# The filler of an attention kernel: hidden units of the MLP dealt between thirds of its second product

## The chip, the cores and the metric

The program runs on one core of one Trainium2 chip. The metric is the device time of one execution in microseconds. An execution of the kernel before was also profiled; the profile holds every instruction of the five engines: TensorE (PE, with its weight loads shown as PEld), VectorE (DVE), ScalarE (ACT), GpSimd (POOL) and SyncE (SP, which issues all DMAs here).

## The reference

`x` is 2048 rows of 640. The rows are normalised, `xn`; attention and an MLP read the same `xn`, and the result joins both:

```python
xn = _layernorm(x, axis=-1)
s = _A_ref(xn, A_wqkv, A_wo)                      # 32 heads of 20, causal window of 256, softmax, then @ wo
g = _silu(_B_ref(xn, B_w1, B_b1, B_w2, B_b2))     # relu(xn @ w1 + b1)**2 @ w2 + b2, hidden width 1536
return x + s * g
```

## The kernel before

All products are done in fp16 with operands split in a high and a low part (high x high, high x low, low x high), so that each product takes three matmuls per tile of the contraction.

**Stages.** A first stage (lines 195 to 529) normalises and transposes x, makes the values of all heads and the first of five groups of 128 q/k rows (each group serves 6.4 heads). Then comes the main loop of 269 steps: 16 pairs of heads times 16 blocks of 128 rows, plus 13 steps in which the last blocks run out. Step s computes the scores of block s (`scores`, L557, 4 matmuls `sps`), their row maxima on DVE (`maxima`, L568), ten steps later the transposed scores (`scores_t`, L604, 4 matmuls `stps` into the one PSUM tile that there is for them), the exponential on ACT (`exps`, L609) with two masking instructions on POOL (L610, L612), one step later its fp16 high part on ACT (`high`, L617), then the low part on DVE (`low`, L623), and every second step 24 small matmuls with the values (`values`, L637, `ops`; 12 of them in the first two blocks of a pair of heads). Last, a tail after the loop does the output product (`out_filler`, tiles `wops`).

**The filler.** The attention of a step leaves TensorE free for most of the step. A generator, `filler()`, gives one matmul at a time with an estimated cost, and `fill(amount)` takes matmuls from it twice in each step until the costs catch up with an even share: `total_` is 423.4 us of cost over 268 steps, 1.58 us a step. The order of the instructions on each engine is the order in which the program issues them (`manual_schedule`), so the order inside `filler()` is the order on TensorE. The filler's work, in this order:

1. q/k groups 1 to 4: for each group g, four column blocks b, and for each of q and k one product of 15 matmuls of 512 columns (`qkps`, cost 0.218 each): 32 units. Each is evacuated by one ACT and one DVE instruction (`qk_parts`, L80 and L81, tile `shm`) and stored by two DMAs.
2. For each of 8 blocks n of 256 rows: 12 hidden units `fc` of 15 matmuls of 256 columns (`hps`, cost 0.111 each), each evacuated by ACT relu (L855), ACT square (L856, tile `hh` high part), DVE square (L858) and POOL subtraction (L859, `hh` low part); then the second product, for two row tiles `tt` and two halves `nh` 36 matmuls of 320 columns (`yps`, cost 0.138 each), evacuated by one DVE instruction (L886).
3. The output product.

Between the hidden units and the second product of a block stands a `flush()`, which issues all evacuations that are pending. Evacuations of a finished product are otherwise pending until the flush in the middle of the next step.

**Weights on the way.** `piece` queues a load of 128 rows of weights into one of `RAW` = 3 buffers and a conversion (`split_s`, L125 on ACT, L126 on DVE) that `tick()` issues at most once a step; a tag in `shut` holds its conversions back, and `ensure(tag)` finishes them at once. Group g + 1 is queued while group g is computed. 17 pieces (`queue_squares`) give sums of squares for the scales of w2 and wo; `second_scales` needs them; then `queue_w2(0)`, `(1)` and, near the end of the q/k groups, `(2)` queue the 12 pieces of w2. w2 lies in three tiles of the pool `bigp`, which has 10 buffers; the third becomes free when the q/k weights `qkw` are no longer read. `queue_wo` queues the five pieces of wo at the start of the last block.

**Buffers.** PSUM pool `pmm` has three banks, shared by `qkps`, `hps` and `yps`. Pool `stgp` has `STG` = 10 buffers, shared by `shm` and the `hh` pairs (two hidden units in one buffer, so six for a block).

Of the kernel before, what the change touches and what calls it, by code (L numbers as in the profile page):

```python
# [7 lines left out]
F32 = mybir.dt.float32  # L8
I32 = mybir.dt.int32
BF16 = mybir.dt.bfloat16  # L10
F16 = mybir.dt.float16
AF = mybir.ActivationFunctionType
# [11 lines left out]
NB = 4  # L24
# [10 lines left out]
LAG = 10  # L35
PB = 6
RATE = 0.9
STG = 10
RAW = 3
EARLY_FILL = 0.35  # L40
SWING = 0.3
# [16 lines left out]
def attn_mlp_kernel(ctx: ExitStack, tc, x, wqkv, wo, w1, b1, w2, b2, out):  # L58
# [20 lines left out]
    def qk_parts(hm, ps):  # L79
        nc.scalar.activation(hm[:, 0, :], ps, AF.Copy, scale=QK_DOWN)  # L80
        nc.vector.scalar_tensor_tensor(hm[:, 1, :], ps, QK_DOWN, hm[:, 0, :], ALU.mult, ALU.subtract)  # L81
# [77 lines left out]
    def lin1(tiles, off, n):  # L159
        t, o = divmod(off, SLOT)  # L160
        return tiles[t][:, o:o + n]
# [370 lines left out]
    at1 = ctx.enter_context(tc.tile_pool(name="at1", bufs=1))  # L532
    qs.append(at1.tile([P, S], F16, name="qs1"))
    ks.append(at1.tile([P, S], F16, name="ks1"))
    at4 = ctx.enter_context(tc.tile_pool(name="at4", bufs=PB))
    at2 = ctx.enter_context(tc.tile_pool(name="at2", bufs=2))

# [125 lines left out]
    def post(dst, src):  # L663
        posts.append((dst, src))
# [9 lines left out]
    def mark():  # L674
        return flushed[0] + len(pending)
# [9 lines left out]
    def mm_group(ps, mms, cost):  # L685
        n = len(mms)
        for j, (a, b_) in enumerate(mms):
            nc.tensor.matmul(ps, a, b_, start=j == 0, stop=j == n - 1)  # L688
            yield cost
# [54 lines left out]
    def ensure(tag):  # L744
        flush()
        while any(p[0] == tag for p in started) or any(p[0] == tag for p in queue):
            start_pieces()
            for f in release(1, True):
                f()
                held[0] -= 1  # L750
# [21 lines left out]
    def queue_squares():  # L772
        for acc, src in [(ss2[:, f:f + 1], w2[f * P:(f + 1) * P, :]) for f in range(NF)] + [(sso[:, c:c + 1], wo[c * P:(c + 1) * P, :]) for c in range(KC)]:
            def go(raw, acc=acc):
                nc.scalar.activation(unread, raw, AF.Square, accum_out=acc)
            piece("s", src, go)

    def weighted_squares():
        g2 = col("m_g2", NF)
        nc.gpsimd.tensor_mul(g2, ss2, mlp["ic4"])  # L780
        mlp["g2"] = g2

    def second_scales():
        s2, i2 = weight_scale("w2", totals("w2_t", pmm.tile([P, NF], F32, tag="mm", name="sums2"), mlp["g2"]))
        so, io = weight_scale("wo", totals("wo_t", pmm.tile([P, KC], F32, tag="mm", name="sumso"), sso))
        sf = col("m_sf", NF)
        nc.vector.tensor_scalar(sf, mlp["ic2"], s2, None, ALU.mult)
        iw = col("o_inv")
        nc.gpsimd.tensor_mul(iw, io, mlp["iv"])
        nc.gpsimd.tensor_scalar(iw, iw, 1.0 / (XS * V_DOWN), 1.0, ALU.mult, ALU.mult)  # L790
        mlp.update(s2=sf, i2=i2, so=so, io=iw)
# [3 lines left out]
    def queue_w2(j):  # L795
        def go(raw, f):
            if len(w2t) == j:
                w2t.append(bigp.tile([P, SLOT], F16, tag="big", name=f"w2_{j}"))
            hi, lo = (lin1(w2t, (2 * f + q) * D, D) for q in range(2))
            split_s(hi, lo, raw, mlp["s2"][:, f:f + 1])  # L800
        for f in range(4 * j, 4 * j + 4):
            piece(f"2{j}", w2[f * P:(f + 1) * P, :], lambda raw, f=f: go(raw, f))

    def filler():
        ws = {1: {w: tuple(qkw[0][:, 1, i, j] for j in range(2)) for i, w in enumerate("qk")}}
        for g in range(1, KC):
            ensure(f"g{g}")
            for b in range(NB):
                if g + 1 < KC and b == 0:
                    ws[g + 1] = queue_group(g + 1)  # L810
                    shut.add(f"g{g + 1}")
                if b == 1:
                    shut.discard(f"g{g + 1}")
                    if g == 1:
                        queue_squares()
                if g == KC - 2 and b == 2:
                    ensure("s")
                    weighted_squares()
                if g == KC - 2 and b == 3:
                    second_scales()  # L820
                    queue_w2(0)
                    queue_w2(1)
                if g == KC - 1 and b == 2:
                    queue_w2(2)
                    shut.add("22")
                for w in "qk":
                    hi, lo = ws[g][w]
                    ps = pmm.tile([P, BT], F32, tag="mm", name="qkps")
                    yield from mm_group(ps, [(wt[:, c, :], xT[b][:, part, c, :]) for c in range(KC) for wt, part in ((hi, 0), (hi, 1), (lo, 0))], 0.218)

                    def evac(ps=ps, w=w, g=g, b=b):
                        hm = stg.tile([P, 2, BT], F16, tag="stg", name="shm")
                        qk_parts(hm, ps)
                        posts.extend(qk_stores(w, slice(g * P, (g + 1) * P), slice(b * BT, (b + 1) * BT), hm))
                    pending.append(evac)
        shut.discard("22")
        nblk = S // MT
        for n in range(nblk):
            if n == nblk - 1:
                wo_part = queue_wo()  # L840
                shut.add("o")
            xb = xT[n // 2][:, :, :, n % 2 * MT:(n % 2 + 1) * MT]
            hs = []
            for fc in range(NF):
                ps = pmm.tile([P, MT], F32, tag="mm", name="hps")
                yield from mm_group(ps, [(lin1(w1t, (2 * c + wp) * F + fc * P, P), xb[:, xp, c, :]) for c in range(KC) for wp, xp in ((0, 0), (0, 1), (1, 0))], 0.111)
                if fc % 2 == 0:
                    pair = stg.tile([P, 2, 2, MT], F16, tag="stg", name="hh")
                hh = pair[:, fc % 2]
                hs.append(hh)  # L850

                def evac(ps=ps, hh=hh, fi=fc):
                    at_f = slice(fi, fi + 1)
                    r = at2.tile([P, MT], F32, tag="relu", name="relu")
                    nc.scalar.activation(r, ps, AF.Relu, bias=mlp["bc"][:, at_f], scale=mlp["a"][:, at_f])  # L855
                    nc.scalar.activation(hh[:, 0], r, AF.Square)  # L856
                    sq = at2.tile([P, MT], F32, tag="sq", name="sq")
                    nc.vector.tensor_mul(sq, r, r)  # L858
                    nc.gpsimd.tensor_sub(hh[:, 1], sq, hh[:, 0])  # L859
                pending.append(evac)  # L860
            if n == nblk - 1:
                shut.discard("o")
            flush()
            if n == 0:
                for j in range(3):
                    ensure(f"2{j}")
            for tt in range(2):
                t = n * 2 + tt
                ysb = wgt.tile([P, D], F32, tag="ysb", name="ysb")
                pss = [pmm.tile([P, HALF], F32, tag="mm", name="yps")]  # L870
                steps_ = []
                for nh in range(2):
                    sl = slice(nh * HALF, (nh + 1) * HALF)
                    for fc in range(NF):
                        steps_.append((max(fc - NF + 3, 0) if tt == 0 else 0, nh, fc, sl))
                if tt == 0:
                    steps_.sort(key=lambda z: z[0])
                for _, nh, fc, sl in steps_:
                    if nh and len(pss) == 1:
                        pss.append(pmm.tile([P, HALF], F32, tag="mm", name="yps"))  # L880
                    for j, (hp, wp) in enumerate(((0, 0), (0, 1), (1, 0))):
                        nc.tensor.matmul(pss[nh], hs[fc][:, hp, tt * P:(tt + 1) * P], lin1(w2t, (2 * fc + wp) * D + nh * HALF, HALF), start=fc == 0 and j == 0, stop=fc == NF - 1 and j == 2)  # L882
                        yield 0.138

                    def evac(ps=pss[nh], ysb=ysb, sl=sl, nh=nh, t=t):
                        nc.vector.scalar_tensor_tensor(ysb[:, sl], ps, mlp["i2"], b2t[:, sl], ALU.mult, ALU.add)  # L886
                        if nh:
                            post(y_d[:, t, :], ysb)
                    if fc == NF - 1:
                        pending.append(evac)  # L890
                if n == nblk - 1:
                    load(0)
                    load(1)
        ensure("o")
        yield from out_filler(wo_part)

# [203 lines left out]
```

## Time and profile before

| | |
|---|---|
| median of 3 runs | 849.37 us (849.28 to 849.63) |
| the profiled execution's own time | 848.83 us |
| its span, first to last instruction | 847.0 us |
| main loop, first to last exponential | 141.5 to 762.2 us |
| q/k groups 1 to 4 on TensorE | 118.9 to 281.2 us |
| hidden units and second products | 281.2 to 767.5 us |
| output product and end | 767.5 to 847.0 us |
| busy time of PE, DVE, ACT, POOL | 822.7, 692.8, 648.1, 485.0 us |

The busy time of a matmul in these records runs from its start to a modelled end, so that consecutive matmuls overlap and a stage can show TensorE busy throughout though its matmuls stand further apart than they need. The distance from start to start is the better measure; the prediction works with it. A row of the stage view reads: the stretch, its length, then for each engine the busy microseconds and the number of instructions, the granted TensorE clock, the DMA engines' busy share and GB/s.

### The profile page before, as it was taken

Reading aid. Unit: us, or ns where it says so; the run is one execution under the profiler, and the core shown is the slowest. Engines: PE = TensorE matmul, PEld = TensorE weight load, DVE = VectorE, ACT = ScalarE, POOL = GpSimd, SP = SyncE. Lnnn points to the kernel's source line nnn. Section 1 sums busy time; section 2 is a strip of 40 time slices with the busy share of each in tenths; the row PEclk is TensorE's granted clock in tenths of the full one; section 3 lists DMA queues with packets and bytes.
Section 4 is the critical chain, followed back from the end, with each engine's and each line's share of the span. In section 5 each row is a group of like instructions: output and inputs, shape, how many; then the busy total and the mean of one; then the engine's idle time right before and its main releaser. Section 6 shows DMA issues by size and latency. Waiting matters only on the chain.

```text
span 847.0 us, 25061 instructions
## 1 busy us (share of the span) xinstructions
PE 822.7 (97%) x9426; PEld 553.4 (65%) x9426; DVE 692.8 (82%) x1897; ACT 648.1 (77%) x1028; POOL 485.0 (57%) x874
## 2 busy tenths in 40 slices
PE   8999998999999999999999999999999999999998
PEld 7765553444444676776766766766767767767775
DVE  6776566788999998898988998888988888975655
ACT  5565446998898997897997997987987988993321
POOL 2000001456665798796896986886986977961000
PEclk9999999999999999999999999999999999999999
DMA  7994349755475311213111222113122113055883
GB/s 245 250 349 129 135 127 283 234 162 157 127 229 163 111 44 55 66 33 89 51 49 50 65 52 65 50 33 84 30 76 65 49 42 99 11 180 171 301 297 126
DMA packets 100498, 104.52 MB, mean 123 GB/s; under 512 B 42520, under 2 KB 72856, under 8 KB 100376
## 3 DMA queue, kind: packets, MB, share of 16 engines
q1 hardware_dynamic: 100376, 102.91, 39.8%
q8 instruction: 74, 1.21, 0.6%
q14 instruction: 48, 0.39, 0.2%
HBM read 65.67 MB, written 36.83 MB: 121 GB/s over the span
## 4 chain that ended last, share of the span: by engine, by line
PE 60%; ACT 14%; POOL 8%; DVE 7%; issue 6%; DMA 3%; SPq 1%; DVEq 0%; ACTq 0%; POOLq 0%
PE yps L882 17%; PE wops L688 8%; PE vps L292 7%; PE hps L688 6%; ACT p L609 5%; PE ops L637 5%; PE qkps L688 5%; PE sps L557 4%; ACT ph L617 3%; PE qkps L503 3%; DVE junk L568 3%; PE stps L604 2%; POOL hh L859 2%; DVE pl L623 2%; ACT relu L855 2%
## 5 line engine op out<-in xcount | busy, mean ns | idle before, releaser
L609 ACT ACTIVATE p<-stps,ebias,esc 128x768 f32<-128x768 f32 (+2 forms) x256 | 242.1, 946 | 59.7 <-PE stps L604 48.9
L568 DVE CUSTOM_DVE_ANT_0 junk<-sps,mask 128x320 bf16<-128x320 f32 (+2 forms) x512 | 220.8, 468 | 49.0 <-PE sps L557 41.4
L623 DVE TENSOR_TENSOR pl<-p,ph 128x768 f16<-128x768 f32 (+2 forms) x256 | 248.8, 972 | 3.8 <-ACT ph L617 3.2
L610 POOL TENSOR_SCALAR_AFFINE_SELECT p<-p 128x256 f32<-128x256 f32 x256 | 163.8, 640 | 86.0 <-ACT p L609 76.7
L617 ACT ACTIVATE ph<-p 128x768 f16<-128x768 f32 (+2 forms) x256 | 203.1, 793 | 2.4 <-POOL p L612 1.6
L688 PE MATMUL hps<-xT,w 128*128 128x256 f16 x1440 | 176.2, 273 | 0.0
L882 PE MATMUL yps<-w,hh 128*128 128x320 f16 x1152 | 174.6, 300 | 0.0
L688 PEld LDWEIGHTS <-w 128*128 128x128 f16 x1440 | 132.6, 98 | 36.0 <-issue 17.2
L882 PEld LDWEIGHTS <-hh 128*128 128x128 f16 x1152 | 104.7, 98 | 57.0 <-issue 18.1
L688 PE MATMUL qkps<-xT,qkw 128*128 128x512 f16 x480 | 115.4, 380 | 0.5 <-DVE w_t L153 0.5
L612 POOL TENSOR_SCALAR_AFFINE_SELECT p<-p 128x256 f32<-128x256 f32 x224 | 103.6, 463 | 0.0
L557 PE MATMUL sps<-ks,qs 60*64 60x320 f16 (+2 forms) x1024 | 87.4, 312 | 6.8 <-DVE mt L568 5.9
L637 PE MATMUL ops<-vp,ph 128*128 128x41 f16 x1440 | 89.8, 181 | 0.0
L637 PE MATMUL ops<-vp,pl 128*128 128x41 f16 x1440 | 89.5, 180 | 0.0
L637 PEld LDWEIGHTS <-ph 128*128 128x128 f16 x1440 | 84.5, 96 | 6.2 <-issue 0.6
L604 PE MATMUL stps<-qs,ks 62*64 62x320 f16 (+4 forms) x1024 | 80.9, 293 | 6.7 <-ACT p L609 6.1
L573 POOL CAST mp<-mt 128x8 f16<-128x8 f32 x64 | 44.6, 698 | 70.0 <-DVE mt L568 69.7
L637 PEld LDWEIGHTS <-pl 128*128 128x128 f16 x1440 | 78.9, 96 | 5.6
L859 POOL TENSOR_TENSOR hh<-sq,hh 128x256 f16<-128x256 f32 x96 | 74.9, 782 | 6.4 <-DVE sq L858 4.3
L688 PEld LDWEIGHTS <-qkw 128*128 128x128 f16 x480 | 41.6, 98 | 55.4 <-issue 11.7
L292 PE MATMUL vps<-wv,xT 128*128 128x320 f16 x480 | 70.3, 303 | 3.2 <-ACT xT L261 1.6
L557 PEld LDWEIGHTS <-qs 60*64 60x64 f16 x1024 | 32.5, 103 | 55.2 <-issue 47.4
(150 smaller groups left out, 1032.4 us busy)
## 6 DMA issues: line engine op xcount, KB each, us to landing
ks<-k_d SPq DMA_DIRECT2D x64, 120.0 KB
qs<-q_d SPq DMA_DIRECT2D x64, 120.0 KB
raw<-in_B_w_dram SPq DMA_DIRECT2D x24, 320.0 KB
v_d<-vt SPq DMA_DIRECT2D x8, 656.0 KB
vp<-v_d SPq DMA_DIRECT2D x16, 328.0 KB
xt<-in_A_x_dram SPq DMA_DIRECT2D x16, 320.0 KB
k_d<-shm SPq DMA_DIRECT2D x20, 256.0 KB
q_d<-shm SPq DMA_DIRECT2D x20, 256.0 KB
```

Source lines behind the costliest of these rows:

```text
L292: nc.tensor.matmul(ps, xT[b][:, xp, c, t * P:(t + 1) * P], wv[wp][:, c, nh * HALF:(nh + 1) * HALF], start=n == 0, stop=n == 3 * KC - 1)
L557: nc.tensor.matmul(ps[HB * j:HB * (j + 1), :nk], qs[i][rows_, q0:q0 + HB], ks[i][rows_, k0:k0 + nk], start=True, stop=True)
L568: nc.vector.tensor_tensor_reduce(out=junk[:, :nk], in0=ps[:, :nk], in1=mk, scale=1.0 / MAX_UNIT, scalar=-3.0e38, op0=ALU.add, op1=ALU.max, ...
L604: nc.tensor.matmul(ps[HB * j:HB * (j + 1), hh, c0:c1], ks[i][rows_, kb * P + HB * j:kb * P + HB * (j + 1)], qs[i][rows_, kb * P + c0:kb * ...
L609: nc.scalar.activation(p32[:, :, :n], ps[:, :, :n], AF.Exp, scale=esc[0], bias=ebias)
L610: nc.gpsimd.affine_select(p32[:, :, 0:P], p32[:, :, 0:P], pattern=[[0, 2], [1, P]], compare_op=ALU.is_ge, fill=0.0, base=0, channel_multip ...
L612: nc.gpsimd.affine_select(p32[:, :, 2 * P:], p32[:, :, 2 * P:], pattern=[[0, 2], [-1, P]], compare_op=ALU.is_gt, fill=0.0, base=0, channel ...
L617: nc.scalar.activation(ph[:, :, :n], p32[:, :, :n], AF.Copy)
L623: nc.vector.tensor_sub(pl[:, :, :n], p32[:, :, :n], ph[:, :, :n])
L637: nc.tensor.matmul(ot[:, q % 4, hh, :], t[:, hh, (q - k) * P:(q - k + 1) * P], vp[:, k // 4, k % 4, hh, :], start=m == 1, stop=m == 2 * le ...
L688: nc.tensor.matmul(ps, a, b_, start=j == 0, stop=j == n - 1)
L882: nc.tensor.matmul(pss[nh], hs[fc][:, hp, tt * P:(tt + 1) * P], lin1(w2t, (2 * fc + wp) * D + nh * HALF, HALF), start=fc == 0 and j == 0, ...
```

## The change

The filler becomes a list of units that is built first and run in that order:

- the first 16 q/k units (groups 1 and 2) come alone, as before;
- the other 16 (groups 3 and 4) alternate with the 12 hidden units of block 0;
- then the 12 hidden units of block n + 1 alternate with 12 *thirds* of the second product of block n (a third is 12 of the 36 matmuls of one accumulation: four of the twelve `fc`), so that an accumulation stays open in its PSUM bank while hidden units run between its thirds;
- the last block's second product comes alone.

Each unit's matmuls and evacuation are the same as before. Before a third, the evacuations are flushed as far as the hidden units that it reads. The pool of staging buffers goes from 10 to 12. The third w2 tile gets a pool of its own (`w2p`), so that all 12 w2 pieces are queued together, after `second_scales`; `weighted_squares` and `second_scales` come at column blocks 0 and 1 of group 3 in place of 2 and 3. `load(0)` and `load(1)` are called ahead of every unit of the last second product.

```diff
-STG = 10
+STG = 12
...
+    w2p = ctx.enter_context(tc.tile_pool(name="w2p", bufs=1))
...
-                w2t.append(bigp.tile([P, SLOT], F16, tag="big", name=f"w2_{j}"))
+                w2t.append(w2p.tile([P, SLOT], F16, name=f"w2_{j}") if j == 2 else bigp.tile([P, SLOT], F16, tag="big", name=f"w2_{j}"))
...
+    def group_unit(g, b, w):
...
+            if g == KC - 2 and b == 0:
+                ensure("s")
+                weighted_squares()
+            if g == KC - 2 and b == 1:
+                second_scales()
+                for j in range(3):
+                    queue_w2(j)
...
+    def out_unit(n, tt, nh, third):
...
+        fs = range(third * THIRD, (third + 1) * THIRD)
+        flush(ready_h[n, fs[-1]])
+        if third == 0:
+            if nh == 0:
+                outs[t] = wgt.tile([P, D], F32, tag="ysb", name="ysb")
+            outs[t, nh] = pmm.tile([P, HALF], F32, tag="mm", name="yps")
+        ps, ysb = outs[t, nh], outs[t]
+        for fc in fs:
+            hh = hidden[n, fc // 2][:, fc % 2]
+            for j, (hp, wp) in enumerate(((0, 0), (0, 1), (1, 0))):
+                nc.tensor.matmul(ps, hh[:, hp, tt * P:(tt + 1) * P], lin1(w2t, (2 * fc + wp) * D + nh * HALF, HALF), start=fc == 0 and j == 0, stop=fc == NF - 1 and j == 2)
+                yield 0.138
...
+    def merge(*lists):
+        items = [((k + 0.5) / len(l), i, u) for i, l in enumerate(lists) for k, u in enumerate(l)]
+        return [u for _, _, u in sorted(items, key=lambda z: z[:2])]
+
+    def filler():
+        groups = [(group_unit, g, b, w) for g in range(1, KC) for b in range(NB) for w in "qk"]
+        hid = [[(hidden_unit, n, fc) for fc in range(NF)] for n in range(nblk)]
+        mlp2 = [[(out_unit, n, tt, nh, third) for tt in range(2) for nh in range(2) for third in range(3)] for n in range(nblk)]
+        half = len(groups) // 2
+        units = groups[:half] + merge(groups[half:], hid[0])
+        for n in range(nblk - 1):
+            units += merge(hid[n + 1], mlp2[n])
+        units += mlp2[-1]
+        for u in units:
+            if u[:3] == (hidden_unit, nblk - 1, 0):
                 wo_part = queue_wo()
                 shut.add("o")
...
+            if u[:2] == (out_unit, nblk - 1):
                 shut.discard("o")
...
+                load(0)
+                load(1)
+            yield from u[0](*u[1:])
```

More of the change, by code (lines that the diff above doesn't have):

```diff
@@ L802, in queue_w2 @@
             piece(f"2{j}", w2[f * P:(f + 1) * P, :], lambda raw, f=f: go(raw, f))
[L804 to L809, printed above, removed]
+    nblk = S // MT
+    hidden, ready_h, outs = {}, {}, {}
+    ws = {1: {w: tuple(qkw[0][:, 1, i, j] for j in range(2)) for i, w in enumerate("qk")}}
+    def group_unit(g, b, w):
+        if w == "q":
+            if b == 0:
+                ensure(f"g{g}")
+                if g + 1 < KC:
@@ L810, in filler @@
                     ws[g + 1] = queue_group(g + 1)
                     shut.add(f"g{g + 1}")
[L812 to L839, printed above, removed]
+            if b == 1:
+                shut.discard(f"g{g + 1}")
+                if g == 1:
+                    queue_squares()
+            if g == KC - 2 and b == 0:
[5 more added lines that the diff above has]
+                    queue_w2(j)
+        hi, lo = ws[g][w]
@@ new lines, in group_unit, with evac, hidden_unit @@
+        ps = pmm.tile([P, BT], F32, tag="mm", name="qkps")
+        yield from mm_group(ps, [(wt[:, c, :], xT[b][:, part, c, :]) for c in range(KC) for wt, part in ((hi, 0), (hi, 1), (lo, 0))], 0.218)
+        def evac():
+            hm = stg.tile([P, 2, BT], F16, tag="stg", name="shm")
+            qk_parts(hm, ps)
+            posts.extend(qk_stores(w, slice(g * P, (g + 1) * P), slice(b * BT, (b + 1) * BT), hm))
+        pending.append(evac)
+    def hidden_unit(n, fc):
+        xb = xT[n // 2][:, :, :, n % 2 * MT:(n % 2 + 1) * MT]
+        ps = pmm.tile([P, MT], F32, tag="mm", name="hps")
+        yield from mm_group(ps, [(lin1(w1t, (2 * c + wp) * F + fc * P, P), xb[:, xp, c, :]) for c in range(KC) for wp, xp in ((0, 0), (0, 1), (1, 0))], 0.111)
+        def evac():
+            if fc % 2 == 0:
+                hidden[n, fc // 2] = stg.tile([P, 2, 2, MT], F16, tag="stg", name="hh")
+            hh = hidden[n, fc // 2][:, fc % 2]
+            at_f = slice(fc, fc + 1)
+            r = at2.tile([P, MT], F32, tag="relu", name="relu")
+            nc.scalar.activation(r, ps, AF.Relu, bias=mlp["bc"][:, at_f], scale=mlp["a"][:, at_f])
+            nc.scalar.activation(hh[:, 0], r, AF.Square)
+            sq = at2.tile([P, MT], F32, tag="sq", name="sq")
+            nc.vector.tensor_mul(sq, r, r)
+            nc.gpsimd.tensor_sub(hh[:, 1], sq, hh[:, 0])
+        pending.append(evac)
+        ready_h[n, fc] = mark()
@@ new lines, in attn_mlp_kernel, with evac @@
+    THIRD = NF // 3
+    def out_unit(n, tt, nh, third):
+        if (n, tt, nh, third) == (0, 0, 0, 0):
+            for j in range(3):
+                ensure(f"2{j}")
+        t = n * 2 + tt
+        sl = slice(nh * HALF, (nh + 1) * HALF)
+        fs = range(third * THIRD, (third + 1) * THIRD)
[6 more added lines that the diff above has]
+        for fc in fs:
+            hh = hidden[n, fc // 2][:, fc % 2]
+            for j, (hp, wp) in enumerate(((0, 0), (0, 1), (1, 0))):
+                nc.tensor.matmul(ps, hh[:, hp, tt * P:(tt + 1) * P], lin1(w2t, (2 * fc + wp) * D + nh * HALF, HALF), start=fc == 0 and j == 0, stop=fc == NF - 1 and j == 2)
+                yield 0.138
+        def evac():
+            nc.vector.scalar_tensor_tensor(ysb[:, sl], ps, mlp["i2"], b2t[:, sl], ALU.mult, ALU.add)
+            if nh:
+                post(y_d[:, t, :], ysb)
+        if third == 2:
+            pending.append(evac)
@@ L840, in filler @@
                 wo_part = queue_wo()
                 shut.add("o")
[L842 to L860, printed above, removed]
@@ L861, in filler @@
-            if n == nblk - 1:
-                shut.discard("o")
[L863 to L893, printed above, removed]
```

## The prediction

> **What bounds the kernel now.** I read the page's head first, then the stretches of the loop, the timeline of TensorE inside two of them, and the waits.
>
> ```profile
> span 847.0 us, 25061 instructions
> PE 822.7 (97%) x9426; PEld 553.4 (65%) x9426; DVE 692.8 (82%) x1897; ACT 648.1 (77%) x1028; POOL 485.0 (57%) x874
> PEclk9999999999999999999999999999999999999999
> ```
>
> TensorE is busy 97% of the span at full clock, so only matmuls that stand further apart than they need can be won. Whether they do is seen stage by stage: six stretches, in order one block of hidden units, two of second products, q/k groups without and with w2 conversions, and the start of block 0's hidden units, with the last four w2 conversions among them.
>
> ```profile
> 465.00:495.60 30.60, 30.13 (x422) 23.15 (x420) 28.19 (x79) 29.26 (x49) 28.20 (x46) 1.00 0.18 48
> 502.30:525.50 23.20, 23.20 (x305) 15.28 (x304) 19.10 (x60) 18.09 (x22) 16.13 (x30) 1.00 0.23 63
> 562.90:586.10 23.20, 23.20 (x306) 15.34 (x305) 18.76 (x58) 16.82 (x22) 15.12 (x30) 1.00 0.25 63
> 264.00:281.00 17.00, 17.00 (x193) 7.96 (x190) 14.48 (x45) 14.66 (x21) 11.69 (x24) 1.00 0.71 211
> 236.00:258.00 22.00, 19.92 (x215) 9.64 (x211) 21.58 (x51) 20.61 (x30) 13.04 (x23) 1.00 0.64 191
> 281.00:296.00 15.00, 13.39 (x195) 10.44 (x192) 14.70 (x36) 14.79 (x23) 11.59 (x17) 1.00 0.35 95
> ```
>
> With hidden units ACT is busy 29.26 of 30.60 us (96%), DVE and POOL 92%; with second products ACT is at 18.09 of 23.20 (78%), DVE 82%, POOL 70%. So the load swings, and in one kind of block ACT runs with no reserve. What this does to TensorE:
>
> ```profile
> 571.75 0.33 PE L557 MATMUL sps<-ks,qs 60*64 60x320 f16 x4
> 571.91 0.31 PE L604 MATMUL stps<-qs,ks 62*64 62x320 f16 x4
> 572.15 1.40 PE L882 MATMUL yps<-w,hh 128*128 128x320 f16 x9
> ...
> 484.19 0.33 PE L557 MATMUL sps<-ks,qs 60*64 60x320 f16 x4
> 484.81 0.33 PE L604 MATMUL stps<-qs,ks 62*64 62x320 f16 x4 [0.29 <-ACT p L609]
> 485.08 1.37 PE L688 MATMUL hps<-xT,w 128*128 128x256 f16 x11
> ```
>
> From the scores to the filler's next matmul TensorE takes 0.40 us among second products, 0.89 among hidden units: the transposed scores have one PSUM tile and wait for the exponential of the step before, which is late on ACT. To add up such losses I take out of a long stretch what its matmuls need. Their distances: the runs below, less one duration, over the gaps; the last two rows are the first and last of the 24 value matmuls of one step.
>
> ```profile
> L688 PE MATMUL hps<-xT,w x1440: 272/273/283, 281.2 to 738.2; 128*128 128x256 f16 x180
> L882 PE MATMUL yps<-w,hh x1152: 296/299/310, 313.9 to 767.3; 128*128 128x320 f16 x192
> ...
> 482.23 2.03 PE L688 MATMUL hps<-xT,w 128*128 128x256 f16 x17
> 574.48 2.08 PE L882 MATMUL yps<-w,hh 128*128 128x320 f16 x14
> 211.23 0.18 PE L637 MATMUL ops<-vp,ph 128*128 128x41 f16 x1
> 211.81 0.18 PE L637 MATMUL ops<-vp,pl 128*128 128x41 f16 x1
> ```
>
> `hps` (2.03 - 0.273) / 16 = 0.110; `yps` (2.08 - 0.299) / 13 = 0.137; `ops` 0.58 / 23 = 0.025 us. Now the counts in six pairs of blocks (342.82 to 706.58) and in one calm run of second products, each cut just behind a score: by line, L604 (four to a step), L637, L882, L688.
>
> ```profile
> 342.82:706.58 363.76, 46.84 (x608) 21.22 (x604) 1.00 0.21 57
> 502.15:525.40 23.25, 3.08 (x44) 1.16 (x40) 1.00 0.23 63
> ...
> 342.82:706.58 363.76, 54.36 (x1680) 53.38 (x1680) 1.00 0.21 57
> 502.15:525.40 23.25, 3.53 (x108) 3.46 (x108) 1.00 0.23 63
> ...
> 342.82:706.58 363.76, 131.06 (x863) 78.39 (x863) 1.00 0.21 57
> 502.15:525.40 23.25, 17.22 (x114) 10.34 (x114) 1.00 0.23 63
> ...
> 342.82:706.58 363.76, 132.26 (x1080) 99.44 (x1080) 1.00 0.21 57
> ```
>
> The weight loads give 604 / 4 = 151 and 40 / 4 = 10 steps. Calm: 23.25 - 114 x 0.137 - 108 x 0.025 = 4.93 us, 0.49 a step. Long: 363.76 - 1080 x 0.110 - 863 x 0.137 - 1680 x 0.025 = 84.7 us, 0.56 a step. The difference, 0.068 a step, is 10.3 us in 151 steps: what TensorE loses to late neighbours there. No more is to be had than that.
>
> **The change, part by part.** *Alternating hidden units with thirds.* The same 96 hidden units, the same second products cut in 96 thirds, the same evacuations: nothing is added on any engine. What goes is the flush of all pending evacuations between the two kinds; a third flushes only as far as it reads, and what it reads is ready for two units or more. A unit of 15 x 0.110 = 1.65 us now stands beside a third of 12 x 0.137 = 1.64, so that a step of 1.58 us of filler meets about one hidden unit in every second step. The shares of a mixed stretch are those of rows one and two together, over 53.8 us: ACT 47.35 (88%), DVE 47.29 (88%), POOL 44.33 (82%). A unit costs ACT the first and second of these rows, DVE the third, POOL the fourth:
>
> ```profile
> L855 ACT ACTIVATE relu<-hps,m,m x96: 546/553/567, 287.1 to 740.9; 128x256 f32<-128x256 f32 x96
> L856 ACT ACTIVATE hh<-relu 128x256 f16<-128x256 f32 x7 | 2.9, 417 | 0.2
> L858 DVE TENSOR_TENSOR sq<-relu x96: 404/540/928, 288.6 to 741.6; 128x256 f32<-128x256 f32 x96
> L859 POOL TENSOR_TENSOR hh<-sq,hh x96: 663/669/1467, 289.3 to 742.1; 128x256 f16<-128x256 f32 x96
> ```
>
> ACT gets 0.97 us more in a step with a unit. In a calm step of 2.33 us it idles 22%, 0.51 us, so two steps, with one unit between them, hold 1.02 us of idle time for 0.97. A step with a unit makes ACT 0.46 us late and the next one takes it back, where twelve units in a row let it grow. TensorE notices only lateness above what a step leaves beside the exponential, 2.33 - 0.95 = 1.4 us:
>
> ```profile
> L609 ACT ACTIVATE p<-stps,ebias,esc 128x768 f32<-128x768 f32 (+2 forms) x256 | 242.1, 946 | 59.7 <-PE stps L604 48.9
> ```
>
> Bounds: all of the loss goes (10.3) or none (0). I take three quarters: 0.46 is well below 1.4, but units do not fall on every second step exactly and DVE and POOL lie at 88 and 82% beside ACT: 7.7 us in the stretch. It stands for 363.8 us; the mixed order runs from 312 (where block 0's hidden units end) to 738 (the last hidden units), 426 us, so 7.7 x 426 / 363.8 = **-9.0 us**. After that the next limit is TensorE itself.
>
> *Groups 3 and 4 among block 0's hidden units, w2's third buffer.* At 1.58 us a step, groups 1 and 2 (16 x 3.27 us) end at step 33 as now, the mixed part (16 x 3.27 + 12 x 1.67) at step 79, as block 0's hidden units do now. What changes inside: the four conversions of w2's last tile come directly behind the other eight and the two of group 4, 14 in a row, each 0.83 us of ACT and 0.88 of DVE.
>
> ```profile
> L125 ACT ACTIVATE w<-raw,m_sf x12: 813/826/847, 235.9 to 291.6; 128x640 f16<-128x640 f32 x12
> L126 DVE SCALAR_TENSOR_TENSOR w<-raw,m_sf,w x12: 869/881/1074, 236.8 to 292.6; 128x640 f16<-128x640 f32 x12
> L80 ACT ACTIVATE shm<-qkps x40: 577/588/647, 80.3 to 282.0; 128x512 f16<-128x512 f32 x40
> ```
>
> Now: among q/k groups (fourth row of the stretches) DVE idles 15% of 2.33 us, 0.34, so a conversion a step overflows by 0.54: eight of them 4.3 us. Among hidden units ACT idles 4%, 0.10, overflow 0.73: four of them 2.9. Together 7.2, with TensorE visibly short in the fifth and sixth rows. After: a step holds 0.26 hidden units (0.25 us of ACT) and 0.13 fewer q/k evacuations (0.08), so ACT idles 14% of 2.33 = 0.32, less 0.17: 0.15, and a conversion overflows by 0.68: 14 make 9.5, less what the lead of the first two takes up (group 4's two cost nothing today): 12 x 0.68 = 8.1. Net **+0.9 us**; bounds -3 (the hidden units, now thinner, give their stall back besides) and +3 (nothing taken up by leads, DVE late as well). The moved loads are 320 KB each on SP's queue; the DMA engines are 64% busy in that stretch. q/k stores come up to 13 steps later (step 79 for the last); group 3 is first read for pair 9, whose load is issued at step 130, so no load waits.
>
> *The rest at nothing.* Twelve staging buffers hold six pairs of each of two blocks; the first pairs come free after the tenth third, before the sixth pair of the next block is asked for. The scales' arithmetic moves, with its one wait (the row below, 0.5 us), which it keeps. The last block's second product and wo's five conversions stay where they are, as does the tail. `load(0)` comes a few steps earlier; nobody waits for it.
>
> ```profile
> PE qkps L688 <- DVE w_t L153: 0.5, 1, 0.5
> ```
>
> Sum against the profiled execution's 848.83: -9.0 + 0.9 = -8.1, 840.7; the median of the runs is 0.5 above that execution, so **841.3 us**.
>
> **The rivals.** *Everything goes (0.10).* All 12 us of 426 us and the merged part at -1: 836 to 837. For it: calm runs show no loss at all; against: 88% shares with in-order queues.
>
> *DVE and POOL get in each other's way in every step (0.13).* `sq` takes 404 ns or up to 928, `hh` 663 or up to 1467: they lengthen when they meet. If each of the 84 units that now alternate met such a neighbour once more, DVE would be busy 84 x 0.52 = 44 us longer, on 88% of 426 = 375: 98%, and the stalls would stay in smaller pieces: 847 to 849. Against: the same units stand today in steps where POOL is at 92%. The Trainium skill's page "SBUF — State Buffer", section "SBUF: two separate sides", says that GpSimd and two-input VectorE operations hold a shared port pair exclusively, the other blocking for the whole instruction; the spread of those two rows agrees, and by that rule alternation trades long collisions for frequent ones.
>
> *The order does not matter (0.08).* The loss belongs to a unit, wherever it stands: 849. Against: the 0.40 and 0.89 us above.
>
> *PSUM (0.07), slower.* An accumulation now holds one of three banks over five units, and hidden units alternate between two. The matmuls of a unit wait for the relu of the last but one. Between them lie two thirds and a unit, 4.9 us of filler, 3.1 steps, 7.2 us; the evacuation takes up to a step to be issued and then an exponential, a high part and 0.55 us, under 5 us. From 2.5 us of lateness on ACT it decides. Lateness now, from the waits between 312 and 742 us:
>
> ```profile
> PE stps L604 <- ACT p L609: 3.0, 10, 0.7
> ```
>
> Ten waits of 0.3 us on average, 0.7 at most. If each of the 84 alternating units waited 0.3 us, that is +25; less the 8.1 that is won elsewhere, 866. Against: those 0.7 us are far from 2.5.
>
> **How the numbers follow.** Forecast 0.62 (837 to 845), everything 0.10, collisions 0.13 (half of it still faster), order 0.08, PSUM 0.07. The range from 836 to 848 leaves out the PSUM case, most of the order case and the edges. About 0.2% (1.7 us) is what can be told from no change: faster 0.62 + 0.10 + 0.07 = 0.79, same 0.06 + 0.08 = 0.14, slower 0.07.
>
> **What would show it.** Right: between 345 and 738 us the time from scores to filler is 0.40 us nearly always, the same sum gives about 0.51 a step in place of 0.56, ACT near 88 to 90% in every stretch, no wait of TensorE for ACT's exponential; around 220 to 255 us a run of 14 steps near 3.0 us. Wrong: `hps` waiting for `relu` (PSUM), long `hh` and `sq` in every step (collisions), or the merged part growing past 3 us.

## The result, and the profile after

| | before | after |
|---|---|---|
| median of 4 runs each, same chip | 849.50 us (849.28 to 850.77) | 837.11 us (836.37 to 837.25) |
| ratio, 95% interval | | 0.9849 (0.9832 to 0.9866) |
| the profiled execution's own time | 848.83 us | 837.25 us |
| its span | 847.0 us | 835.5 us |

The changed kernel is 12.4 us faster by the medians, 11.6 us by the two profiled executions. One of the four runs of the kernel in which only the MLP alternates (further down) took 997.62 us at a mean granted clock of 0.75; its figures are those of the three other runs, and its profile, which shows that run, is not read. In the changed kernel's code the lines have moved: L558 is `sps`, L569 the maxima, L605 `stps`, L610 the exponential, L689 `hps` and `qkps`, L848 to L852 the evacuations of a hidden unit, L874 `yps`.

The head of its page, in the same order as before:

```profile
span 835.5 us, 24908 instructions
PE 815.3 (98%) x9426; PEld 548.1 (66%) x9426; DVE 686.0 (82%) x1897; ACT 648.5 (78%) x1028; POOL 476.9 (57%) x874
PEclk9999999999999999999999999999999999999999
```

The numbers of matmuls, and the busy time of ACT, are those of before. "97%" has become "98%": the head hardly shows a gain of 1.4%, because a matmul's busy time runs to a modelled end and covers part of the distance to the next.

The stage view shows more. The columns are: stretch, length, then busy time (instructions) of PE, PEld, DVE, ACT and POOL, granted clock, DMA share, GB/s. The first row is nearly the whole mixed part; the other two are the stretches in which the kernel before ran a block of hidden units and one of second products.

```profile
345.00:735.00 390.00, 390.00 (x5367) 279.88 (x5366) 346.60 (x1015) 351.64 (x536) 318.16 (x560) 1.00 0.21 58
465.00:495.60 30.60, 30.60 (x426) 21.98 (x422) 27.15 (x81) 27.29 (x42) 25.83 (x47) 1.00 0.25 67
502.30:525.50 23.20, 23.20 (x324) 16.69 (x323) 21.51 (x62) 21.64 (x33) 19.39 (x36) 1.00 0.21 56
```

The kernel before, same view and first stretch:

```profile
345.00:735.00 390.00, 386.14 (x5261) 278.75 (x5254) 343.93 (x998) 343.45 (x527) 319.11 (x545) 1.00 0.21 56
```

Its ACT stood at 29.26 of 30.60 us in one kind of block and at 18.09 of 23.20 in the other. Now it stands at 27.29 (89%) and 21.64 (93%): the swing from 96% to 78% has shrunk to 4 points, while the mean has risen (351.64 of 390.00 against 343.45, because the same work is done in less time). TensorE shows no idle time in 390 us and starts 5367 matmuls there in place of 5261.

TensorE's timeline where the kernel before took 0.89 us from the scores to the filler's next matmul:

```profile
481.67 0.33 PE L558 MATMUL sps<-ks,qs 60*64 60x320 f16 x4
481.83 0.31 PE L605 MATMUL stps<-qs,ks 62*64 62x320 f16 x4
482.07 0.58 PE L874 MATMUL yps<-w,hh 128*128 128x320 f16 x3
482.49 0.93 PE L689 MATMUL hps<-xT,w 128*128 128x256 f16 x7
483.94 0.33 PE L558 MATMUL sps<-ks,qs 60*64 60x320 f16 x4
484.11 0.31 PE L605 MATMUL stps<-qs,ks 62*64 62x320 f16 x4
484.35 1.05 PE L689 MATMUL hps<-xT,w 128*128 128x256 f16 x8
485.23 0.98 PE L874 MATMUL yps<-w,hh 128*128 128x320 f16 x6
```

It is 0.40 us (481.67 to 482.07) and 0.41 us (483.94 to 484.35), the time that only calm steps had, and a step's filler now holds both kinds.

The sum of the prediction, made again: counts between two cuts just behind a score, by line L605, L638, L874 and L689.

```profile
345.94:711.23 365.29, 46.87 (x624) 18.16 (x628) 1.00 0.21 59
345.94:711.23 365.29, 56.67 (x1752) 55.65 (x1752) 1.00 0.21 59
345.94:711.23 365.29, 145.31 (x888) 81.14 (x888) 1.00 0.21 59
345.94:711.23 365.29, 146.79 (x1118) 103.30 (x1117) 1.00 0.21 59
```

628 / 4 = 157 steps. 365.29 - 1117 x 0.110 - 888 x 0.137 - 1752 x 0.025 = 76.9 us, **0.49 a step**. Before it was 0.56, in the calm run 0.49, and 0.51 was forecast: to this precision nothing of the loss is left.

### The profile page after: what moved, and what is told of

It is laid out like the page before. It is cut to its first block, busy times and chain, and to the rows that moved or that the text cites. A ratio compares the mean times of both kernels' runs of the same rounds, so it can differ in the third digit from the quotient of the medians.

```text
span 835.5 us, 24908 instructions
## 1 busy us (share of the span) xinstructions
PE 815.3 (98%) x9426; PEld 548.1 (66%) x9426; DVE 686.0 (82%) x1897; ACT 648.5 (78%) x1028; POOL 476.9 (57%) x874
## 4 chain that ended last, share of the span: by engine, by line
PE 82%; ACT 7%; DVE 5%; issue 3%; DMA 2%; SPq 0%; DVEq 0%; ACTq 0%
PE hps L689 19%; PE yps L874 19%; PE wops L689 8%; PE ops L638 7%; PE vps L292 7%; PE sps L558 7%; PE qkps L689 7%; PE stps L605 3%; PE qkps L503 3%; ACT p L610 2%; DVE junk L569 2%; ACT ph L618 1%; PE otp L956 1%; PE tps L256 1%; DVE pl L624 1%
## 5 line engine op out<-in xcount | busy, mean ns | idle before, releaser
L610 ACT ACTIVATE p<-stps,ebias,esc 128x768 f32<-128x768 f32 (+2 forms) x256 | 242.3, 947 | 50.2 <-PE stps L605 42.4
L569 DVE CUSTOM_DVE_ANT_0 junk<-sps,mask 128x320 bf16<-128x320 f32 (+2 forms) x512 | 221.3, 469 | 54.8 <-PE sps L558 44.6
L624 DVE TENSOR_TENSOR pl<-p,ph 128x768 f16<-128x768 f32 (+2 forms) x256 | 243.6, 952 | 4.7 <-ACT ph L618 4.0
L611 POOL TENSOR_SCALAR_AFFINE_SELECT p<-p 128x256 f32<-128x256 f32 x256 | 171.4, 670 | 90.4 <-ACT p L610 87.8
L689 PE MATMUL hps<-xT,w 128*128 128x256 f16 x1440 | 188.8, 273 | 0.0
L874 PE MATMUL yps<-w,hh 128*128 128x320 f16 x1152 | 186.6, 300 | 0.0
L689 PEld LDWEIGHTS <-w 128*128 128x128 f16 x1440 | 133.3, 98 | 43.7 <-issue 23.7
L874 PEld LDWEIGHTS <-hh 128*128 128x128 f16 x1152 | 105.1, 98 | 55.6 <-issue 21.8
L689 PE MATMUL qkps<-xT,qkw 128*128 128x512 f16 x480 | 117.0, 381 | 0.8 <-DVE w_t L153 0.8
L613 POOL TENSOR_SCALAR_AFFINE_SELECT p<-p 128x256 f32<-128x256 f32 x224 | 110.5, 493 | 0.0
L558 PE MATMUL sps<-ks,qs 60*64 60x320 f16 (+2 forms) x1024 | 86.1, 313 | 6.5 <-DVE mt L569 5.9
L638 PE MATMUL ops<-vp,ph 128*128 128x41 f16 x1440 | 89.8, 181 | 0.0
L638 PE MATMUL ops<-vp,pl 128*128 128x41 f16 x1440 | 89.5, 181 | 0.0
L638 PEld LDWEIGHTS <-ph 128*128 128x128 f16 x1440 | 84.6, 96 | 6.2 <-issue 0.6
L638 PEld LDWEIGHTS <-pl 128*128 128x128 f16 x1440 | 78.9, 96 | 5.8
L605 PE MATMUL stps<-qs,ks 62*64 62x320 f16 (+4 forms) x1024 | 79.6, 291 | 2.3 <-ACT p L610 2.0
L689 PEld LDWEIGHTS <-qkw 128*128 128x128 f16 x480 | 41.6, 98 | 53.4 <-issue 11.7
L852 POOL TENSOR_TENSOR hh<-sq,hh 128x256 f16<-128x256 f32 x96 | 67.6, 704 | 13.0 <-DVE sq L851 9.3
L689 PE MATMUL wops<-wo,oT 128*128 128x320 f16 x480 | 66.7, 299 | 0.8 <-ACT oT L121 0.8
```

The costliest lines, as they stand in the source:

```text
L558: nc.tensor.matmul(ps[HB * j:HB * (j + 1), :nk], qs[i][rows_, q0:q0 + HB], ks[i][rows_, k0:k0 + nk], start=True, stop=True)
L569: nc.vector.tensor_tensor_reduce(out=junk[:, :nk], in0=ps[:, :nk], in1=mk, scale=1.0 / MAX_UNIT, scalar=-3.0e38, op0=ALU.add, op1=ALU.max, ...
L605: nc.tensor.matmul(ps[HB * j:HB * (j + 1), hh, c0:c1], ks[i][rows_, kb * P + HB * j:kb * P + HB * (j + 1)], qs[i][rows_, kb * P + c0:kb * ...
L610: nc.scalar.activation(p32[:, :, :n], ps[:, :, :n], AF.Exp, scale=esc[0], bias=ebias)
L611: nc.gpsimd.affine_select(p32[:, :, 0:P], p32[:, :, 0:P], pattern=[[0, 2], [1, P]], compare_op=ALU.is_ge, fill=0.0, base=0, channel_multip ...
L613: nc.gpsimd.affine_select(p32[:, :, 2 * P:], p32[:, :, 2 * P:], pattern=[[0, 2], [-1, P]], compare_op=ALU.is_gt, fill=0.0, base=0, channel ...
```

## The experiments

Two theories of where the gain lies. *Lateness*: in a run of hidden units ACT and DVE fall behind a little with each unit, until TensorE waits; alternation keeps them from it. *Boundary*: the flush between the two kinds of block costs, and the new order has no such flush. Beside them stands the question of what the other half of the change, groups 3 and 4 among block 0's hidden units, is worth. All edits are to the changed kernel. Ratios are to the kernel before, run on the same chip in the same session. The experiments were timed in three sessions on three chips, so between sessions ratios are compared, not times; "by the ratios" below means a difference of ratios times 850 us.

### Either half alone

Only the MLP alternates; all q/k groups come first:

```diff
-        units = groups[:half] + merge(groups[half:], hid[0])
+        units = groups + hid[0]
```

> The change without its first part: the twelve hidden units of block 0 come alone behind all q/k groups; the alternation of hidden units and thirds, the third w2 buffer and the earlier scales stay. Lateness theory (ACT and DVE fall behind from hidden unit to hidden unit and TensorE waits once they are more than about 1.4 us late): the whole gain is in the alternation, so 836 to 838 us; the conversions of w2 stand among q/k groups alone at an overflow of about 0.54 us each in place of 0.68, which takes about 1.5 us off, and block 0's hidden units lose about 1.2 us as a loaded block does. Rival (the mixing of groups 3 and 4 with block 0 is part of the gain): 839 to 842 us.

Measured: 837.38 us, 0.9858 (0.9834 to 0.9881). That can't be told from the whole change.

Only the groups are merged; each block's second product is again in one piece behind its hidden units:

```diff
-            units += merge(hid[n + 1], mlp2[n])
+            units += mlp2[n] + hid[n + 1]
```

> The change without its second part: groups 3 and 4 alternate with block 0's hidden units, w2 has its third buffer and the scales come early, but each second product comes whole behind its own block's hidden units, ahead of the next block's. Lateness theory: the gain is gone and the merged part costs about 1 us, so 849 to 852 us, with the sum of losses of about 0.56 us a step back in 345 to 738 us. Rival (the merged part and the early conversions bring part of the gain): 844 to 847 us.

Measured: 849.56 us, 0.9994 (0.9983 to 1.0006). Its stage view over the long stretch, and its row of the waits between 345 and 730 us (who waits, for whom, total us, times, longest):

```profile
345.00:735.00 390.00, 386.43 (x5269) 279.29 (x5270) 344.26 (x997) 343.85 (x527) 319.69 (x547) 1.00 0.21 57
```

```profile
PE stps L605 <- ACT p L610: 3.3, 10, 0.7
```

Both are the picture of before: 386.43 busy microseconds, and ten waits for the exponential. As far as the intervals tell, the whole gain lies in the alternation; the flushes as far as a third reads, the thirds themselves and the merged groups bring nothing without it.

### How long may a run of one kind be?

```diff
+    def runs(k, a, b):
+        return [u for i in range(0, len(a), k) for u in a[i:i + k] + b[i:i + k]]
...
-            units += merge(hid[n + 1], mlp2[n])
+            units += runs(k, hid[n + 1], mlp2[n])
```

With k = 12 a block of hidden units runs whole, but the second product behind it reads the block before: nothing in it has to wait for what was just computed, so the boundary should be harmless and lateness is what is left.

> Hidden units and thirds in runs of two, to complete the row of run lengths (1: 0.985 of before, 3: 0.988, 6: 0.9925, 12: 0.997). An accumulation is open across some runs, but no more than two hidden units stand beside it, one in each of the two banks left. Lateness theory: 2 x 0.46 = 0.9 us, below what a step leaves, so 837 to 838.5 us. If open accumulations cost in themselves, 841 us or more.

> Hidden units and thirds in runs of three. Three thirds are one whole accumulation, so no PSUM bank is held open while hidden units run, as one was in the runs of four, where TensorE waited for the relu (5.8 us in nine waits). If those waits cost the runs of four most of their time, runs of three are at 837 to 839 us: lateness of 3 x 0.46 = 1.4 us is just what a step leaves. If lateness of ACT and DVE alone decides and its limit is lower than I worked out, 842 to 847 us.

> The change with hidden units and thirds alternating in runs of four units and four thirds. Lateness theory: each unit makes ACT about 0.46 us later and a run of four reaches 1.8 us, 0.4 above what a step leaves, so each of 21 runs loses 0.1 to 0.4 us: 839 to 845 us. Boundary theory (the loss came from second products that stand directly behind their own hidden units, with all evacuations flushed between): 837 us, as here every third still reads hidden units of a block before.

> Runs of six, two whole accumulations each, again no bank held open. Lateness theory: 6 x 0.46 = 2.8 us, above the 1.4 that a step leaves, so a loss in each of 14 runs, less than in runs of twelve (847.0 us): 841 to 846 us. PSUM theory (only open accumulations cost): 837 to 839 us.

> The same in runs of twelve: all hidden units of block n + 1, then the whole second product of block n. Lateness theory: the loaded stretches are as long as before, so nearly all of the gain is gone: 846 to 850 us. Boundary theory: no second product stands behind its own hidden units and nothing is flushed at once, so the gain stays: 837 to 839 us.

| units of one kind in a row | us | ratio, 95% interval |
|---|---|---|
| 1 (the change) | 837.11 | 0.9849 (0.9832 to 0.9866) |
| 2 | 838.14 | 0.9853 (0.9835 to 0.9872) |
| 3 | 839.78 | 0.9882 (0.9867 to 0.9898) |
| 4 | 848.21 | 0.9982 (0.9971 to 0.9993) |
| 6 | 843.11 | 0.9925 (0.9908 to 0.9941) |
| 12 | 846.98 | 0.9969 (0.9956 to 0.9982) |

Apart from k = 4, the ratio rises with the length (1 and 2 can't be told apart), and a run of 12 gives back four fifths of the gain though no second product stands behind its own hidden units there: lateness, and some 2.6 us (849.56 to 846.98, timed together) for what a boundary may cost besides. k = 2, 6 and 12 lie in the ranges of the lateness theory; k = 3 lies 0.8 us above its first range. The k = 12 kernel's stages show the swing again; 376 to 406 us is a run of hidden units there:

```profile
350.00:380.00 30.00, 30.00 (x394) 20.28 (x390) 25.61 (x78) 23.96 (x33) 21.09 (x39) 1.00 0.21 59
380.00:410.00 30.00, 29.58 (x406) 22.30 (x404) 27.29 (x78) 28.52 (x47) 26.43 (x45) 1.00 0.20 56
410.00:440.00 30.00, 29.75 (x390) 19.95 (x386) 24.61 (x76) 23.52 (x33) 20.96 (x39) 1.00 0.18 49
```

ACT goes from 80% to 95% and back to 78%. TensorE's waits for the exponential come back with the length; between 345 and 730 us the kernel with k = 6 and then that with k = 12 show:

```profile
PE stps L605 <- ACT p L610: 1.4, 4, 0.5
```

```profile
PE stps L605 <- ACT p L610: 2.5, 9, 0.4
```

These are 1.4 and 2.5 us where some 6.5 and 10 us are lost by the ratios: a named wait counts only the time in which no modelled matmul runs. The rest is in distances between matmuls, which this view doesn't show. The prediction's sum does; for k = 12, with the lines in the same order as after the change:

```profile
344.70:708.58 363.88, 46.62 (x608) 21.02 (x608) 1.00 0.22 60
344.70:708.58 363.88, 55.10 (x1707) 54.13 (x1704) 1.00 0.22 60
344.70:708.58 363.88, 131.72 (x864) 78.39 (x864) 1.00 0.22 60
344.70:708.58 363.88, 133.00 (x1090) 100.48 (x1090) 1.00 0.22 60
```

608 / 4 = 152 steps; 363.88 - 1090 x 0.110 - 864 x 0.137 - 1704 x 0.025 = 83.0 us, 0.55 a step. The same sum over nearly the same stretch gives 0.50 for k = 2 and 3, 0.53 for k = 6, and 0.55 for the kernel with the groups alone.

The starts of all matmuls in the traces, between 343 and 709 us, tell where in a step the loss stands. From the last matmul of the scores to the first of the transposed scores, which wait for the exponential, it is 144 ns on average in the change; 147, 150, 174 and 186 ns in runs of 2, 3, 6 and 12; and 186 in the kernel before. So about 42 of the 68 ns a step that the kernel before loses stand in front of the transposed scores, behind ACT; the rest is spread over several distances, none of them above 9 ns a step.

### Runs of four: a PSUM bank held open

k = 4 missed both expectations (839 to 845, and 837 us) on the slow side. Its waits of TensorE between 312 and 738 us:

```profile
PE hps L689 <- ACT relu L848: 6.7, 10, 1.2
```

That is not the wait for an exponential but the one for a free PSUM bank, the prediction's own PSUM rival. An accumulation has three thirds; four thirds in a row end, two times out of three, inside the next accumulation, whose bank is then held while four hidden units run on the two that are left. Runs of 1 and 2 hold a bank too, but with no more hidden units in a row than there are banks left. The test: the same four hidden units in a row, but thirds only in whole accumulations.

```diff
-            units += merge(hid[n + 1], mlp2[n])
+            h, o = hid[n + 1], mlp2[n]
+            units += h[0:4] + o[0:3] + h[4:8] + o[3:6] + h[8:12] + o[6:12]
```

> Runs of four hidden units again, but each followed by three thirds (one whole accumulation; six behind the last run), so that no accumulation is open while hidden units run. PSUM theory (the runs of four lost to TensorE waiting for a bank, 848.2 us): between the runs of three and of six, 839.5 to 843 us, and no wait of hps for relu. If run length alone makes the 848.2, it stays at 846 to 849 us.

Measured: 839.53 us, 0.9873 (0.9858 to 0.9888). All of its waits of TensorE between 312 and 738 us:

```profile
PE stps L605 <- ACT p L610: 0.2, 1, 0.2
PE sps L558 <- DVE mt L569: 0.2, 1, 0.2
```

The waits for `relu` are gone, and 0.9982 has become 0.9873: by the ratios the open bank cost about 9 us. The traces place it: between 343 and 709 us the mean distance from one `hps` matmul to the next is 118 ns with the open bank and 110 ns without, 8 us over 998 of them. With the accumulations whole, runs of 4 can't be told from runs of 3 (0.9882).

### The merged part: w2's conversions spaced

In the change the conversions come one a step, and TensorE idles for 4 of the 38 us around them. Here w2's pieces are taken up only in every third step:

```diff
     def tick():
...
+        if started and started[0][0] in ("20", "21", "22") and state[2] % 3:
+            return
```

> The changed kernel with the twelve conversions of w2 issued at every third step in place of every step, over nearly the whole merged part. In 222 to 260 us DVE is busy 37.95 of 38 us, and behind it, without conversions, 87%, so a step leaves it 0.30 us and three steps 0.9 for a conversion of 0.88. If the rest of the loss in the merged part (about 7 us) is the bunching of the conversions, 830 to 833 us. If it lies in the merging itself or in other waits there, 836 to 838 us.

Measured: 834.40 us (833.65 to 835.38), 0.9820 (0.9806 to 0.9835), the fastest of all. The change, and then the spaced kernel, in two stretches of that part:

```profile
222.00:260.00 38.00, 34.02 (x383) 19.20 (x381) 37.95 (x94) 36.61 (x55) 28.95 (x42) 1.00 0.61 188
264.00:312.00 48.00, 48.00 (x589) 27.55 (x587) 41.91 (x126) 41.66 (x64) 34.20 (x63) 1.00 0.35 99
```

```profile
222.00:260.00 38.00, 37.38 (x435) 20.41 (x434) 35.96 (x100) 35.90 (x54) 29.91 (x49) 1.00 0.53 160
264.00:312.00 48.00, 47.36 (x565) 26.65 (x564) 47.00 (x129) 45.68 (x69) 38.55 (x62) 1.00 0.43 130
```

TensorE wins 3.4 us of busy time in the first stretch (435 matmuls in place of 383) and gives 0.6 back in the second, where DVE is now at 47.00 of 48.00 (98%). TensorE's waits between 221 and 312 us, in the change and then in the spaced kernel:

```profile
PE sps L558 <- DVE mt L569: 3.7, 7, 0.8
```

```profile
PE sps L558 <- DVE mt L569: 0.6, 3, 0.2
```

The scores waited for the maxima, which stood behind the conversions on DVE, and 3.1 us of that are gone. In its median the kernel is 2.7 us below the change, but the two were timed in different sessions and their intervals overlap. It lies between the two ranges that were expected (830 to 833, 836 to 838). That DVE, with no reserve in the second stretch, spreads part of the loss rather than losing it would explain this; no run shows it.

Spacing with the groups not merged (the diffs of the first and of this experiment together):

> The same spacing without the merging of groups 3 and 4 with block 0 (hidden units of block 0 alone behind all groups). The conversions stand among q/k groups, the last three or four of them among hidden units, where ACT has no reserve. If the merging is of use once the conversions are spaced, this is 1 to 4 us above the kernel that has both; if not, equal to it within 1 us.

Measured: 835.84 us, 0.9836 (0.9821 to 0.9850), 1.4 us above the spaced kernel, with overlapping intervals. So with the conversions spaced, merging shows 1.4 us, which the intervals don't settle.

### Without w2's third buffer

w2's third tile goes back into the shared pool, so its four pieces can be queued only after the last q/k unit, which now stands near the end of the merged part:

```diff
-                w2t.append(w2p.tile([P, SLOT], F16, name=f"w2_{j}") if j == 2 else bigp.tile([P, SLOT], F16, tag="big", name=f"w2_{j}"))
+                w2t.append(bigp.tile([P, SLOT], F16, tag="big", name=f"w2_{j}"))
...
-                for j in range(3):
+                for j in range(2):
                     queue_w2(j)
...
+            if u == groups[-1]:
+                queue_w2(2)
```

> The changed kernel with the third w2 tile back in the common pool, its four pieces queued when the last q/k group is issued, since the pool has no free buffer earlier. In the merged order that is only one hidden unit ahead of the first third, so their loads and conversions are finished at once there. Against that, ten and not fourteen conversions stand in a row. If the buffer matters, 839 to 846 us, with TensorE idle around 312 us for the loads; if not, 836 to 838 us.

Measured: 844.76 us, 0.9935 (0.9915 to 0.9955), some 7 us above the change by the ratios. Its profiled execution took 846.95 us, 9.7 us more than that of the change. Two rows of its waits between 300 and 340 us:

```profile
PE sps L584 <- DVE mt L569: 7.8, 1, 7.8
...
ACT w L125 <- DMA raw<-in_B_w_dram: 4.5, 3, 2.1
```

One wait is most of the loss. `ensure` finishes the late conversions at once, ACT waits 4.5 us for their loads, and the step's maxima on DVE stand behind them in order. No run has the third buffer in the old order; with the groups merged alone it is there, and nothing is gained (0.9994). In the new order it is what brings the weights in time.

## Why the prediction was right, step by step

- **The bound and the mechanism** held. TensorE's distances, not its busy share, carried the gain; the loss of 0.068 us a step came from how the load on its neighbours was ordered, and went with the order. Run lengths 1 to 12 show it as a scale, and the half change without alternation shows none of the gain. The size was off: 837.11 us is 4.2 under the 841.3 that was forecast, at the lower edge of its 837 to 845.
- **The term that was mis-sized is "I take three quarters" (-9.0).** All of it went: 0.49 us a step against 0.56. With 10.3 in place of 7.7, scaled by the same 426 / 363.8, the term is -12.1; with the +0.9 kept, 848.83 - 11.2 = 837.6 against 837.25 measured. The reason for the discount, that units don't fall on every second step exactly and that DVE and POOL lie beside ACT, rested on shares (88 and 82%) but on no row that gives it a price. The prediction's own row spoke for more: 0.46 us of lateness against a margin of 1.4 leaves room for a second and even a third unit in a row, and by the ratios runs of 2 and 3 indeed lose only 0.3 and 2.8 us. "Everything goes", at 836 to 837, was closer.
- **The margin of 1.4 us** is borne out only roughly. At 0.46 us a unit, runs of 2, 3, 4, 6 and 12 would be 0.9, 1.4, 1.8, 2.8 and 5.5 us late at their end. By the ratios they cost 0.3, 2.8, 2.0 (accumulations whole), 6.5 and 10.2 us in all over the change. Nothing that can be told is lost at 2 and clearly something at 6, but no sharp point is seen at which it starts. Most of the loss stands behind ACT's exponential, as the prediction had it; how much of ACT's lateness comes from what it gets late from DVE, no run separated.
- **The merged groups, +0.9 us**, were small, as forecast, but their exact price stays open. The conversions after the change (count, min/median/max ns, first and last start):

```profile
L126 DVE SCALAR_TENSOR_TENSOR w<-raw,m_sf,w x12: 862/871/1297, 224.9 to 257.2; 128x640 f16<-128x640 f32 x12
```

  Twelve in 32.3 us, 32.3 / 11 = 2.94 us a step where 3.0 was forecast. And the start of the second products:

```profile
L874 PE MATMUL yps<-w,hh x1152: 296/299/311, 317.3 to 755.8; 128*128 128x320 f16 x192
```

  317.3 against 313.9 before, 3.4 us later. A hidden unit of block 1 now stands ahead of it, 1.65 us of filler in steps of 2.33 us for 1.58, so 2.4 us; by this estimate the other 1.0 us is the cost. The kernel with the groups alone has no hidden unit ahead of its first `yps` and starts it at 316.7, 2.8 us later than before, yet its whole time is that of before within an interval of -1.4 to +0.5 us. All of this lies in the forecast's bounds of -3 and +3. The last `yps` is 11.5 us earlier than before, nearly the whole difference, so the tail stayed as it was.
- **Edits at nothing.** The staging buffers caused no wait that shows, and TensorE waited for nothing between 312 and 738 us. The third w2 buffer had no price of its own in the sum; taken away, it costs some 7 us.
- **The collisions rival** fell. The groups of POOL's subtraction, before and then after (busy us, mean ns, idle before):

```profile
L859 POOL TENSOR_TENSOR hh<-sq,hh 128x256 f16<-128x256 f32 x96 | 74.9, 782 | 6.4 <-DVE sq L858 4.3
```

```profile
L852 POOL TENSOR_TENSOR hh<-sq,hh 128x256 f16<-128x256 f32 x96 | 67.6, 704 | 13.0 <-DVE sq L851 9.3
```

  The mean fell from 782 to 704 ns, where alternation was to make such meetings more frequent. The Trainium skill's page "SBUF — State Buffer", section "SBUF: two separate sides", says that GpSimd and two-input VectorE operations block each other for a whole instruction; the rows speak neither for nor against that, but frequent meetings, which the rival drew from it, did not come.
- **"The order does not matter"** fell with the run lengths. **PSUM** did not decide in the change, where no `hps` waits for `relu`: as the prediction had argued, two thirds and a unit lie between a bank's filling and its reuse. But it was a real mechanism with a near edge: the runs of 4 met it, and there it took about 9 us.

## What to carry to other kernels

Where filler work hides behind a fixed pattern, look at the load that each kind of filler puts on the engines that evacuate it, and deal heavy kinds among light ones: one to three units in a row kept 10 to 12 us here, twelve kept under 3. An engine that is busy 88% on average can still cost the bound engine time if it is at 96% in one kind of block and 78% in the next; read the shares by stage, and measure the loss in distances between starts, since named waits showed 3 of some 12 us. When products are cut to be dealt, see how much work runs while each piece holds its accumulation bank, and see that the weights of what comes earlier are there earlier too.

## What the runs showed of the hardware that had not been expected

In the kernel without the third buffer, TensorE's long wait had a price after its end. Its stages, two of them in finer cuts (clock is the third column from the right), and, from the timeline, a hidden unit of 15 matmuls before the wait and one after it:

```profile
315.00:325.00 10.00, 4.74 (x70) 3.44 (x67) 5.89 (x11) 5.95 (x9) 3.94 (x8) 0.83 0.61 182
325.00:335.00 10.00, 7.46 (x77) 4.56 (x77) 6.61 (x20) 6.95 (x10) 5.09 (x9) 0.66 0.29 85
...
321.00:323.00 2.00, 0.00 (x0) 0.00 (x0) 1.00 (x2) 1.53 (x3) 0.00 (x0) 0.66 0.31 122
331.00:333.00 2.00, 2.00 (x18) 1.07 (x17) 0.68 (x3) 0.49 (x1) 0.38 (x1) 0.78 0.24 43
```

```profile
315.41 1.81 PE L689 MATMUL hps<-xT,w 128*128 128x256 f16 x15
...
327.54 0.27 PE L584 MATMUL sps<-identh,mp 128*128 128x128 f16 x1 [7.80 <-DVE mt L569]
...
328.62 3.40 PE L689 MATMUL hps<-xT,w 128*128 128x256 f16 x15
```

The granted clock is 0.83 and 0.66 in the two long stretches and 1.00 in the windows quoted above, and the same 15 matmuls took 3.40 in place of 1.81 us. The Trainium skill's page "TensorE: Matmul & The Clock Gate", section "What's actually happening", says that the gate passes half of the pulses after an idle window of about 3.4 us and all of them again after about 3.4 us of work; a wait of 7.8 us and a unit at nearly half speed behind it agree. The fall came sooner than after 3.4 us without work, though: 0.66 between 321 and 323 us puts it, from 1.00 to the 0.50 of 323 to 325 us, at about 321.6, which is 1.9 us after the wait began (327.54 - 7.80 = 319.74). The rise, by the 0.78 between 331 and 333, came at about 331.9, 4.3 us after its end. So this one long wait of TensorE cost more than its length, 1.6 us more on that unit alone. The ten short waits of the kernel with runs of four, 1.2 us at most, left the clock at 1.00 over their stretch:

```profile
312.00:738.00 426.00, 418.84 (x5715) 298.41 (x5713) 375.20 (x1093) 374.86 (x570) 343.31 (x595) 1.00 0.21 57
```
